# One scale for w_out, batch 0 kept in 32-bit pairs, and PSUM as three shared double banks: attention over packed rows with a SoLU layer

## The chip, the core and the metric

The program runs on one core of a Trainium2 chip. The metric is the time of one execution on the device in microseconds (us), taken as the median of several runs. The engines are named as in the profile: PE is the matmul engine (PEld its weight loads), DVE is VectorE, ACT is ScalarE, POOL is GpSimd, SP issues the DMAs.

## The reference

```python
# q, k, v: (8, 8, 576, 64); p: (8, 8, 32, 64); w_in: (512, 1024); w_out: (1024, 512)
def sm_attn(qq, kk, vv):
    s = scale * np.matmul(qq, kk.transpose(0, 1, 3, 2))
    s = s - np.max(s, axis=-1, keepdims=True)
    a = np.exp(s)
    a = a / (np.sum(a, axis=-1, keepdims=True) + 1e-09)
    return np.matmul(a, vv)
p_packed = sm_attn(p, k, v)              # 32 packed rows for each head
out = sm_attn(q, p_packed, p_packed)     # 576 rows for each head
x = out.transpose(0, 2, 1, 3).reshape(4608, 512)
h = x @ w_in
e = np.exp(h - max(h)); solu = h * e / (sum(e) + 1e-09)
ln = (solu - mean(solu)) / np.sqrt(var(solu) + 1e-06) * g_ln
return ln @ w_out
```

## The kernel before

**Units.** The work of a batch b is cut into flows: `k{b}` (`pack`: scores of the 32 packed rows of each head against the 576 keys, softmax, product with v), `q{b}` (`unpack`: scores of the 576 queries against the packed rows, softmax), and `z{b}` (`make_z`: packed rows times w_in, so that h = a · z needs no x of its own). Tokens are handled in 36 tiles of 128, `t0` to `t35` (`token_tile`): h from 12 matmuls of 512 columns (three for each half of the heads and each half of the columns), row maximum, exponential, the product u, the LayerNorm moments, a transpose by DMA, 24 matmuls into `po`, and the scaling by `c_row` on the way out. Tile 4 of each pair of batches is shared: 64 rows of the even batch and 64 of the odd one, whose matmuls use 64 columns of the array each.

**Numbers.** Products are made from pairs of parts (high·high, high·low, low·high). From batch 1 on the parts are 16-bit (`a_h`, `a_l`, `zh`, `zl`). Batch 0 uses 32-bit pairs (`a_r`, `z_r`) in its first four tiles, since the sizes that the 16-bit scales need are not known so early; for its last 64 rows, in `t4`, flow `y0` (`halves_of_z`) makes 16-bit parts of z afterwards, and `unpack` makes 16-bit parts of the last 64 columns of a.

**Weights.** w_in and w_out arrive as 64-bit words; `W0` to `W3` and `O0` to `O3` rebuild them as 32-bit numbers on ACT, DVE and POOL. For w_out each of the eight parts of 128 rows also gives `mag`, |g · w|, which PE sums over all rows with ones into one bank of 512 columns. `S` (`column_scale`) turns those 512 sums into a scale for each column, and `C0` to `C7` (`scaled_parts`) multiply w_out by g and the scale (DVE), cast the high part (ACT, `wch`) and subtract for the low part (POOL, `wcl`). `N` sizes w_in and `H` (`weight_halves`) makes its 16-bit parts for batches 2 to 7.

**PSUM.** There are eight banks: `ps_h` two tiles of two banks (h of the token tiles, all of batch 0, `p`), `ps_a` three tiles of one bank (scores, transposes and z of batches 1 to 7), `ps_o` one bank (`po`).

**Order.** Each flow is a generator; `ORDER` is a written list of 1372 names, and each name lets its flow issue the next step. Every engine runs its instructions in that order. SP's queue holds all DMAs in that order too. `SCALED_BY`, `E1T_BY` and their like are strings that choose an engine for an operation (a: ACT, d or x: DVE, p or g: POOL).

## Time and profile before

| | |
|---|---|
| median of 3 runs | 406.47 us (406.39 to 407.71) |
| the profiled execution | 406.56 us, of which the span of the instructions is 404.3 us |
| PE busy | 388.4 us (96%) |
| DVE, ACT, POOL busy | 310.4 us (77%), 266.3 us (66%), 241.1 us (60%) |
| granted clock of PE, mean | 0.996 of full speed |

The span is shorter than the time of its execution by 2.2 us, which lie around it. Busy times are of one execution. Matmuls overlap, so PE's busy time is no sum of their durations: 512 columns of 16-bit numbers show 0.38 us and start 0.21 to 0.22 us apart.

### The profile page before, as it was taken

The page shows a single profiled execution, that of the slowest core. Times are in us where ns is not written, and L with a number is a line of the kernel's source. Part 1 is how long each engine was busy: PE and PEld are TensorE (multiplying, and loading weights), DVE is VectorE, ACT ScalarE, POOL GpSimd, SP SyncE. Part 2 cuts the span into 40 slices and gives each one's busy share as a digit, 9 for nine tenths or more (in the row PEclk, how much of TensorE's full clock was granted, in tenths as well). Part 3 has the DMA queues.
Part 4 walks back from the last instruction along what each step waited for, and adds up shares of the span by engine and source line. Part 5 has one row for each costly group of instructions (what it writes and reads, how often), then busy time and mean ns, then how long its engine had stood idle before and what let it go on. Part 6 is the DMA issues. An engine that isn't in the chain of part 4 may idle for free.

```text
span 404.3 us, 8920 instructions
## 1 busy us (share of the span) xinstructions
PE 388.4 (96%) x3378; PEld 196.7 (49%) x3378; DVE 310.4 (77%) x550; ACT 266.3 (66%) x486; POOL 241.1 (60%) x423
## 2 busy tenths in 40 slices
PE   8988988999899999999999999999999999999996
PEld 8764655543433554345345444554455444444445
DVE  0265799999999989877998798888688787566631
ACT  2678998978677764685486844874476566754720
POOL 1442776665647886494548656663487568854450
PEclk9989999999999999999999999999999999999999
DMA  8999792779799995899896879863765354443661
GB/s 297 375 359 346 214 163 44 139 149 198 151 199 175 195 158 111 162 213 191 150 209 131 163 137 219 143 136 83 149 180 109 79 109 100 104 99 80 110 152 56
DMA packets 213865, 66.11 MB, mean 163 GB/s; under 512 B 194744, under 2 KB 207808, under 8 KB 213312
## 3 DMA queue, kind: packets, MB, share of 16 engines
q1 hardware_dynamic: 213824, 65.56, 74.3%
q8 instruction: 26, 0.43, 0.4%
q14 instruction: 15, 0.12, 0.1%
HBM read 37.23 MB, written 9.44 MB: 115 GB/s over the span
## 4 chain that ended last, share of the span: by engine, by line
PE 70%; DVE 12%; ACT 6%; POOL 4%; DMA 3%; SPq 2%; issue 2%; DVEq 0%; POOLq 0%; ACTq 0%
PE po L717 34%; PE h L662 17%; PE h L717 5%; DMA yT<-yhl 2%; PE po L116 2%; SPq L152 2%; PE pa L567 2%; PE pa L504 2%; PE pa L394 2%; DVE u L687 1%; PE pa L424 1%; PE pa L434 1%; ACT u L235 1%; ACT mag L255 1%; DVE kT L377 1%
## 5 line engine op out<-in xcount | busy, mean ns | idle before, releaser
L717 PE MATMUL po<-wch,yT 128*128 128x512 f16 x512 | 160.4, 380 | 0.2 <-DMA yT<-yhl 0.2
L717 PEld LDWEIGHTS <-yT 128*128 128x128 f16 x888 | 84.8, 98 | 103.9 <-issue 9.3
L717 PE MATMUL po<-wcl,yT 128*128 128x512 f16 x256 | 97.1, 379 | 0.0
L687 DVE SCALAR_TENSOR_TENSOR u<-e,s_row,h 128x1024 f32<-128x1024 f32 x36 | 45.8, 1271 | 16.8 <-ACT e L683 7.4
L693 ACT ACTIVATE yhl<-u,negmu 128x1024 f16<-128x1024 f32 x36 | 41.3, 1147 | 21.6 <-POOL negmu L690 21.4
L695 DVE SCALAR_TENSOR_TENSOR yhl<-u,negmu,yhl 128x1024 f16<-128x1024 f32 x36 | 46.3, 1286 | 5.6 <-ACT yhl L693 5.6
L665 DVE TENSOR_REDUCE nm<-h 128x1 f32<-128x1024 f32 x36 | 43.8, 1215 | 7.7 <-PE h L662 7.6
L662 PE MATMUL h<-zl,a_h 128*128 128x512 f16 (+1 forms) x160 | 47.9, 380 | 0.1
L683 ACT ACTIVATE e<-h,nmc,z_scale 128x1024 f32<-128x1024 f32 x32 | 38.4, 1201 | 7.8 <-DVE nmc L668 7.1
L701 ACT ACTIVATE e<-u,negmu 128x1024 f32<-128x1024 f32 x36 | 41.0, 1139 | 0.0
L673 POOL TENSOR_SCALAR bound<-nm,z_scale 128x1 f32<-128x1 f32 x31 | 17.9, 576 | 38.1 <-DVE nm L665 37.1
L662 PEld LDWEIGHTS <-a_h 128*128 128x128 f16 (+1 forms) x288 | 24.1, 101 | 31.5 <-issue 7.7
L662 PE MATMUL h<-zh,a_h 128*128 128x512 f16 (+1 forms) x128 | 38.3, 381 | 0.0
L670 ACT ACTIVATE nmc<-nm,z_scale 128x1 f32<-128x1 f32 x29 | 8.5, 295 | 39.4 <-DVE nm L665 39.2
L722 DVE SCALAR_TENSOR_TENSOR o_sb<-po,c_row,inv 128x512 f32<-128x512 f32 x32 | 23.9, 746 | 12.6 <-PE po L717 8.5
L662 PE MATMUL h<-zl,a_l 128*128 128x512 f16 (+1 forms) x80 | 30.3, 379 | 0.0
L709 POOL TENSOR_TENSOR c_row<-c_row,neg_half 128x1 f32<-128x1 f32 x36 | 23.8, 662 | 3.0
L662 PE MATMUL h<-zh,a_l 128*128 128x512 f16 (+1 forms) x64 | 24.3, 379 | 0.0
L679 POOL TENSOR_TENSOR s_row<-bound,neg_one 128x1 f32<-128x1 f32 x33 | 22.0, 667 | 2.7
L690 POOL TENSOR_SCALAR negmu<-su 128x1 f32<-128x1 f32 x36 | 7.4, 205 | 26.2 <-DVE u L687 22.6
L409 ACT ACTIVATE e<-pa,nmx 128x288 f32<-128x288 f32 x28 | 13.7, 493 | 12.5 <-DVE nmx L400 12.5
L475 POOL TENSOR_TENSOR s<-s,mx 128x576 f32<-128x576 f32 x14 | 17.7, 1278 | 7.0 <-DVE mx L473 6.8
(187 smaller groups left out, 747.2 us busy)
## 6 DMA issues: line engine op xcount, KB each, us to landing
out_dram<-o_sb SPq DMA_DIRECT2D x35, 256.0 KB, 2.6
v_sb<-in_v_dram SPq DMA_DIRECT2D x8, 1024.0 KB, 7.0
raw<-in_k_dram SPq DMA_DIRECT2D x24, 288.0 KB, 4.3
raw<-in_q_dram SPq DMA_DIRECT2D x96, 72.0 KB, 2.5
zl<-in_moe_w_in_dram SPq DMA_DIRECT2D x2, 1024.0 KB, 8.1
zh<-in_moe_w_in_dram SPq DMA_DIRECT2D x2, 1024.0 KB, 8.1
raw<-in_k_dram SPq DMA_DIRECT2D x2, 1024.0 KB, 9.7
raw<-in_q_dram SPq DMA_DIRECT2D x2, 1024.0 KB, 7.5
```

Source lines behind the costliest of these rows:

```text
L662: nc.tensor.matmul(dst_[:, cols], lhsT=lhsT, rhs=z[:, r, cols], start=bool(first), stop=bool(last))
L665: nc.vector.tensor_reduce(out=nm, in_=h, axis=AX.X, op=ALU.max, negate=True)
L673: by.tensor_scalar(out=bound, in0=nm, scalar1=-1.0 / U_MAX, scalar2=sc[:, :1], op0=ALU.mult, op1=ALU.max)
L679: nc.gpsimd.tensor_tensor(out=s_row, in0=bound, in1=neg_one, op=ALU.pow)
L683: nc.scalar.activation(e, h, AF.Exp, bias=nmc, scale=sc[:, 1:], accum_out=se)
L687: nc.vector.scalar_tensor_tensor(out=u, in0=e, scalar=s_row, in1=h, op0=ALU.mult, op1=ALU.mult, accum_out=su)
L693: nc.scalar.activation(yhl[:, 0], u, AF.Identity, bias=negmu)
L695: nc.vector.scalar_tensor_tensor(out=yhl[:, 1], in0=u, scalar=negmu, in1=yhl[:, 0], op0=ALU.add, op1=ALU.subtract)
L701: nc.scalar.activation(e, u, AF.Square, bias=negmu, accum_out=sq)
L709: nc.gpsimd.tensor_tensor(out=c_row, in0=c_row, in1=neg_half, op=ALU.pow)
L717: nc.tensor.matmul(po[:, cols], lhsT=yT[:, a, c], rhs=w[:, c, cols], start=c == 0 and t == 0, stop=c == NFC - 1 and t == 2)
L722: nc.vector.scalar_tensor_tensor(out=o_sb[:, cols], in0=po[:, cols], scalar=c_row, in1=inv[:, cols], op0=ALU.mult, op1=ALU.mult)
```

## The change

- **One scale for w_out.** `mag` becomes a Square on ACT with a sum over its row (`ssq`); the eight matmuls into the shared bank go. `S` sums the eight columns of `ssq` by one small matmul and gets one scale (a power of two) for the whole of w_out; `gs` is g times it, `inv` one number for each partition instead of 512. `C`: ACT makes `wch` straight from w with the scale in it, POOL multiplies w by `gs` and subtracts; DVE has no part in it.
- **Batch 0 in 32-bit pairs to its end.** `t4` uses `a_r` and `z_r` for the 64 rows of batch 0; `y0`, the 16-bit parts of a's last columns and batch 0's size go. `a_r` grows from 512 to 576 columns. `H` puts its high parts into the two buffers of `a_r` (so it follows `t4`'s products) and its low parts in place into w_in; `zh` and `zl` have both buffers for z again.
- **PSUM.** `ps_h` has three tiles of two banks, `ps_a` one bank. Scores, row transposes and z of all batches take a `ps_h` tile.
- **Score rows in `pack`.** One maximum and one exponential over both halves (2 × 288) instead of two of each; two small reduces for each row go. The transposes of the exponentials are evicted as 8 and 2 blocks instead of 4, 4 and 2, always by ACT; those of batch 1's q and k two groups at a time.
- **ORDER** is a new list of 1308 names. What the removed steps leave stays in about the same sequence; among the differences: the w_in part 2 and the keys of batch 0 are loaded first, w_out's part 0 earlier, `H` and `t4` change places.

```diff
-SCALED_BY = 'xxxxxxxx'
+SCALED_BY = 'gggggggg'
-E1T_BY = 'dadaaaaaa'
+E1T_BY = 'aaaaaa'
...
-    ps_h = ctx.enter_context(tc.tile_pool(name='ps_h', bufs=2, space=PSUM))
+    ps_h = ctx.enter_context(tc.tile_pool(name='ps_h', bufs=3, space=PSUM))
-    ps_a = ctx.enter_context(tc.tile_pool(name='ps_a', bufs=3, space=PSUM))
+    ps_a = ctx.enter_context(tc.tile_pool(name='ps_a', bufs=1, space=PSUM))
-    inv = const.tile([P, DM], F32, name='inv')
+    inv = const.tile([P, 1], F32, name='inv')
-    a_r = [par.tile([P, 2, MAIN], F32R, name=f'a_r{i}') for i in range(2)]
+    a_r = [par.tile([P, 2, S], F32R, name='a_r', bufs=2) for i in range(2)]
...
     def convert_w_out(n):
-            nc.tensor.matmul(sums[0], lhsT=ones, rhs=mag, start=len(sums) == 1, stop=len(sums) == NFC)
+            nc.scalar.activation(mag, t[:, i * DM:(i + 1) * DM], AF.Square, scale=g_sb[:, c:c + 1], accum_out=ssq[:, c:c + 1])
...
+    def size_of(dst, parts):
+        ps = ps_a.tile([P, 512], F32, name='pa')
+        n = parts.shape[-1]
+        nc.tensor.matmul(ps[:, :n], lhsT=ones_f, rhs=parts, start=True, stop=True)
+        yield
+        nc.vector.tensor_reduce(out=dst, in_=ps[:, :n], axis=AX.X, op=ALU.add)
+        half_exponent(dst, dst)
+    def w_out_scale():
+        yield from size_of(inv, ssq)
+        up = small.tile([P, 1], F32, name='up')
+        nc.vector.tensor_scalar(out=up.bitcast(I32), in0=inv.bitcast(I32), scalar1=-1, scalar2=204 << 23, op0=ALU.mult, op1=ALU.add)
+        yield
+        nc.vector.tensor_scalar_mul(gs, g_sb, up)
+        nc.vector.tensor_scalar(out=inv.bitcast(I32), in0=inv.bitcast(I32), scalar1=65 << 23, scalar2=None, op0=ALU.add)
...
     def scaled_parts(c):
-            nc.vector.scalar_tensor_tensor(out=w, in0=w, scalar=g_sb[:, c:c + 1], in1=scale[0], op0=ALU.mult, op1=ALU.mult)
...
-        nc.scalar.copy(wch[:, c], w)
...
-        EN(nc, REST_BY[c]).tensor_tensor(out=wcl[:, c], in0=w, in1=wch[:, c], op=ALU.subtract)
+            nc.scalar.activation(wch[:, c], w, AF.Copy, scale=by)
...
+                nc.gpsimd.tensor_scalar(out=w, in0=w, scalar1=by, scalar2=0.0, op0=ALU.mult, op1=ALU.add)
...
+            nc.gpsimd.tensor_tensor(out=wcl[:, c], in0=w, in1=wch[:, c], op=ALU.subtract)
...
     def weight_halves():
+        hi = [par.tile([P, 4 * S], F16, name='a_r', bufs=2)[:, :2 * DF].rearrange('p (g f) -> p g f', g=2) for _ in range(2)]
+        halves.append([hi[g // 2][:, g % 2] for g in range(G)])
+        halves.append([w_in_sb[:, g].bitcast(F16)[:, :DF] for g in range(G)])
...
     def pair(b):
+        t = ps_h.tile([P, DF], F32, name='h')
+        return [t[:, :512], t[:, 512:], t]
...
     def transpose_rows(dst, raw, b, by, m0):
-        wide = 1 if b else 2
+        wide = 2
...
     def pack(b):
+                both = s1[2].rearrange('p (n x) -> p n x', n=2)[:, :, :HALF]
+                nc.vector.tensor_reduce(out=nmx, in_=both, axis=AX.XY, op=ALU.max, negate=True)
+                yield
...
+                nc.scalar.activation(dst, both if by_rows else both.rearrange('p n (a t) -> p n a t', t=32), AF.Exp, bias=nmx, accum_out=ssum[:, r:r + 1])
...
-        for i0 in range(0, len(items), 4):
-            grp = items[i0:i0 + 4]
+        for i0 in range(0, len(items), 8):
+            grp = items[i0:i0 + 8]
+            pt = ps_h.tile([P, DF], F32, name='h') if len(grp) > 4 else ps_a.tile([P, 512], F32, name='pa')
...
     def unpack(b):
-                parts = [(a_r[0][:, r], a_r[1][:, r], a2T[:, :MAIN]), (a_h[0][:, r, MAIN:], a_l[0][:, r, MAIN:], a2T[:, MAIN:])]
+            hi, lo = (a_h[b % 2][:, r], a_l[b % 2][:, r]) if b else (a_r[0][:, r], a_r[1][:, r])
...
-    def halves_of_z():
...
     def token_tile(i, dst, b, c):
+                        a_hi, a_lo, z_hi, z_lo = (a_h[x], a_l[x], zh[c + x], zl[c + x]) if c + x else (a_r[0], a_r[1], z_r[0], z_r[1])
...
-            nc.vector.scalar_tensor_tensor(out=o_sb[:, cols], in0=po[:, cols], scalar=c_row, in1=inv[:, cols], op0=ALU.mult, op1=ALU.mult)
+            nc.vector.tensor_scalar(out=o_sb[:, cols], in0=po[:, cols], scalar1=c_row, scalar2=inv, op0=ALU.mult, op1=ALU.mult)
```

## Rows read from the trace of the kernel before

**Rows 1.** Windows: us, busy of PE, PEld, DVE, ACT, POOL; PEclk, DMA share, GB/s.

```profile
20.00:40.00 20.00, 16.27 (x255) 11.49 (x257) 11.62 (x24) 16.09 (x29) 7.38 (x3) 0.91 1.06 353
40.00:56.00 16.00, 14.09 (x184) 8.91 (x185) 13.01 (x24) 15.88 (x29) 11.50 (x7) 1.00 0.87 198
56.00:78.00 22.00, 19.84 (x221) 12.58 (x216) 21.76 (x43) 20.27 (x45) 15.17 (x18) 1.00 0.62 102
78.00:131.00 53.00, 50.76 (x449) 21.71 (x441) 51.80 (x97) 40.70 (x74) 31.94 (x59) 1.00 0.90 173
131.00:380.00 249.00, 248.70 (x2018) 114.30 (x2011) 200.89 (x352) 158.43 (x293) 160.81 (x303) 1.00 0.70 141
```

**Rows 2.** Instructions of PE in order of time: start, duration, count at the end.

```profile
56.61 0.50 PE L662 MATMUL h<-zh,a_r 128*128 128x512 f32 x1
...
76.86 0.40 PE L662 MATMUL h<-zl,a_r 128*128 128x512 f32 x1
77.10 0.40 PE L662 MATMUL h<-zh,a_r 128*128 128x512 f32 x1
...
78.07 0.39 PE L717 MATMUL po<-wch,yT 128*128 128x512 f16 x1
...
103.06 0.38 PE L662 MATMUL h<-zh,a_h 128*64 128x512 f16 x1
103.06 0.38 PE L662 MATMUL h<-zl,a_h 128*64 128x512 f16 x1
...
232.34 0.59 PE L662 MATMUL h<-zh,a_h 128*128 128x512 f16 x2
```

**Rows 3.** Whom PE waited for from 40 to 131 us: total, times, longest.

```profile
PE pa L441 <- DVE pp L438: 1.8, 2, 1.2
```

**Rows 4.** Groups of PE: busy us, mean ns of one.

```profile
L259 PE MATMUL po<-mag,ones 128*128 128x512 f32 x8 | 4.0, 501 | 1.6 <-ACT mag L255 1.5
```

**Rows 5.** Groups of ACT: busy us, mean ns of one.

```profile
L409 ACT ACTIVATE e<-pa,nmx 128x288 f32<-128x288 f32 x28 | 13.7, 493 | 12.5 <-DVE nmx L400 12.5
L409 ACT ACTIVATION_READ_ACCUMULATOR e<-pa,nmx 128x1 f32 x28 | 5.5, 197 | 0.0
L366 ACT COPY kT<-h 128x1024 f32<-128x1024 f32 x1 | 1.0, 1012 | 3.3 <-PE h L364 3.3
```

**Rows 6.** Groups of DVE: busy us, mean ns of one.

```profile
L695 DVE SCALAR_TENSOR_TENSOR yhl<-u,negmu,yhl 128x1024 f16<-128x1024 f32 x36 | 46.3, 1286 | 5.6 <-ACT yhl L693 5.6
L473 DVE TENSOR_REDUCE mx<-s 128x18 f32<-128x576 f32 x16 | 11.6, 738 | 0.0
L398 DVE TENSOR_REDUCE mx<-pa 128x1 f32<-128x288 f32 x28 | 11.3, 445 | 1.8 <-PE pa L394 1.7
L636 DVE SCALAR_TENSOR_TENSOR zh<-zf,z_scale,zh 128x512 f16<-128x512 f32 x4 | 4.1, 1058 | 0.0
L289 DVE SCALAR_TENSOR_TENSOR yT<-yT,g_sb,po 128x512 f32<-128x512 f32 x4 | 3.0, 740 | 0.0
L400 DVE TENSOR_REDUCE nmx<-mx 128x1 f32<-128x2 f32 x16 | 2.5, 155 | 0.5
L525 DVE TENSOR_TENSOR a_l<-s,a_h 128x64 f16<-128x64 f32 x2 | 1.4, 707 | 0.0
L270 DVE TENSOR_SCALAR po<-po 128x512 f32<-128x512 f32 x1 | 0.7, 700 | 0.1
```

**Rows 7.** Groups of POOL: busy us, mean ns of one.

```profile
L690 POOL TENSOR_SCALAR negmu<-su 128x1 f32<-128x1 f32 x36 | 7.4, 205 | 26.2 <-DVE u L687 22.6 <-DVE s_p L543 3.2 <-DVE ssum L411 0.4
L297 POOL TENSOR_TENSOR wcl<-yT,wch 128x512 f16<-128x512 f32 x4 | 5.5, 1372 | 2.3 <-ACT wch L295 2.3
```

**Rows 8.** Instructions of DVE in order of time, two places.

```profile
97.91 1.77 DVE L636 SCALAR_TENSOR_TENSOR zh<-zf,z_scale,zh 128x512 f16<-128x512 f32 x1
...
238.67 1.28 DVE L687 SCALAR_TENSOR_TENSOR u<-e,s_row,h 128x1024 f32<-128x1024 f32 x1
```

**Rows 9.** An instruction of POOL in order of time.

```profile
96.95 2.18 POOL L525 TENSOR_TENSOR a_l<-s,a_h 128x576 f16<-128x576 f32 x1 [2.35 <-ACT a_h L522]
```

More of the change, by code (lines that the diff above doesn't have):

```diff
@@ L110, in packed_attention_solu_kernel @@
     size, weight, whole, halves = ({}, [], {}, [])
-    got, packed, wg, sums, scale = ({}, {}, {}, [], [])
+    got, packed, wg = ({}, {}, {})
     spare = ps_o.tile([P, DM], F32, name='po')
@@ L180, in prepare_g @@
         yield
-        nc.scalar.copy(g_sb, spare[:, :NFC])
+        nc.scalar.activation(g_sb, spare[:, :NFC], AF.Copy, scale=2.0 ** (-16))
         yield
@@ L313, in weight_size @@
             yield
-        ps = ps_a.tile([P, 512], F32, name='pa')
-        nc.tensor.matmul(ps[:, :G], lhsT=ones_f, rhs=sums_, start=True, stop=True)
-        yield
         w = const.tile([P, 1], F32, name='w_size')
-        nc.vector.tensor_reduce(out=w, in_=ps[:, :G], axis=AX.X, op=ALU.add)
-        half_exponent(w, w)
+        yield from size_of(w, sums_)
         nc.vector.tensor_scalar(out=w.bitcast(I32), in0=w.bitcast(I32), scalar1=-1, scalar2=235 << 23, op0=ALU.mult, op1=ALU.add)
@@ L343, in bank @@
     def bank(b):
-        return ps_a.tile([P, 512], F32, name='pa') if b else ps_h.tile([P, DF], F32, name='h')
+        return ps_h.tile([P, DF], F32, name='h')
     def pair(b):
-        if b == 0:
-            t = bank(b)
-            return [t[:, :512], t[:, 512:]]
-        return [bank(b), bank(b)]
+        t = ps_h.tile([P, DF], F32, name='h')
+        return [t[:, :512], t[:, 512:], t]
     def transpose_rows(dst, raw, b, by, m0):
@@ L445, in pack @@
         yield
+        if not b:
+            return
         squares = att.tile([P, 2 * D], F32, name='squares')
@@ L492, in unpack @@
             for r in range(2):
[L493 removed]
+                for n, bank_ in enumerate(pair(b)[:2]):
                     for out_, lhsT, rhs in scores(bank_, r, n):
@@ L555, in product @@
         def product(n):
-            in_h = not b or Z_IN_H[b] == str(n + 1)
-            if in_h:
-                banks[n] = pair(0)
+            banks[n] = pair(0)[:2]
             cols = slice(512 * n, 512 * n + 512)
             if ZP_BY[b] == '1':
-                if not in_h:
-                    banks[n] = [bank(b), bank(b)]
                 for t, (x, y) in enumerate(((0, 0), (0, 1), (1, 0))):
@@ L566, in product @@
                         for g in range(G):
-                            nc.tensor.matmul(banks[n][r][32 * g:32 * g + 32, :], lhsT=pph[rows, x, 32 * g:32 * g + 32], rhs=halves[y][rows, g, cols], start=t == 0, stop=t == 2)
+                            nc.tensor.matmul(banks[n][r][32 * g:32 * g + 32, :], lhsT=pph[rows, x, 32 * g:32 * g + 32], rhs=halves[y][g][rows, cols], start=t == 0, stop=t == 2)
                 yield
@@ L570, in product @@
             for r in range(2):
-                if not in_h:
-                    banks[n].append(bank(b))
                 rows = slice(64 * r, 64 * r + 64)
@@ L617, in make_z @@
                     yield from part(n)
-    def halves_of_z():
-        z_scale(0)
-        s_z = zsc[0][:, :1]
-        parts = par.tile([P, 2, 2, DF], F16, name='zh', bufs=2)
-        zh[0], zl[0] = (parts[:, 0], parts[:, 1])
-        if 0 not in whole:
-            whole[0] = par.tile([P, 2, DF], F32, name='zf')
-        yield
-        for n in range(2):
-            for r in range(2):
-                cols = slice(512 * n, 512 * n + 512)
-                if ZF_BY[0] == 'l':
-                    nc.gpsimd.tensor_tensor(out=whole[0][:, r, cols], in0=z_r[0].bitcast(F32)[:, r, cols], in1=z_r[1].bitcast(F32)[:, r, cols], op=ALU.add)
-                    yield
-                nc.scalar.activation(zh[0][:, r, cols], whole[0][:, r, cols], AF.Copy, scale=s_z)
-                yield
-                nc.vector.scalar_tensor_tensor(out=zl[0][:, r, cols], in0=whole[0][:, r, cols], scalar=s_z, in1=zh[0][:, r, cols], op0=ALU.mult, op1=ALU.subtract)
-                yield
     def token_tile(i, dst, b, c):
```

84 lines of the change are left out of this document (29 added, 55 removed).

## The prediction

> **What bounds the kernel now.** I read the windows first, to split the span into stages, then PE's waits, then the groups of each engine. After 131 us nothing is left to gain around PE: it is busy 248.70 of 249 us there, so that stage can only become longer, or shorter by the work taken from PE [rows 1]. What can be won lies before. Between 40 and 56 us ACT is full (15.88 of 16), and between 56 and 131 DVE is (21.76 and 51.80 of 75 us, together 73.56); ACT has 60.97 there, POOL 47.11 [rows 1]. PE's idle time is 3.73 us in 20 to 40, 1.91 in 40 to 56, 2.16 in 56 to 78 and 2.24 in 78 to 131 [rows 1]. The first two stages end with the first matmul of the first token tile at 56.61; the first of an output product comes at 78.07 [rows 2]. The longest of PE's waits after 40 us is for DVE's `pp` [rows 3], a 64-column operation behind a full queue, which agrees with DVE as the limit. PE's idle time is a lower bound of what a faster DVE returns, because a matmul shows 0.38 us and the next can start after some 0.22; short waits hide in that.
>
> **The change, part by part.**
>
> *The sums of w_out.* Eight matmuls with 4.0 us of busy time go from PE [rows 4]; one small one comes. They all lie between 32 and 49 us, where PE has idle time and ACT and the loads set the pace, so the removal is worth between 0 (idle time takes their place) and 4.0 (PE had been the limit). DVE loses the three operations of `S` on 512 columns, 3 × 0.70 = 2.1 us [rows 6], and gets eight small ones of at most 0.155 each, 1.2 us.
>
> *ACT before the first tile.* The squares cost what the magnitudes did, plus the read of the accumulator: 8 × 0.197 = 1.6 us more [rows 5]. The eviction of batch 0's transposed exponentials moves from DVE: one copy of 1.01 in place of one half as wide, and a narrow one of at most 0.5, together about 1.0 more. Gone are the copy of `inv` (0.5, half as wide as the 1.01 row), two narrow casts and batch 0's size with its read (four short instructions, 0.8 at 0.197 each), and in each of its two score rows two exponentials with their reads, 2 × (0.493 + 0.197) = 1.38 us, for one of 576 columns that costs between 0.69 and 2 × 0.493 + 0.197 = 1.18 [rows 5]: 0.4 to 1.4 less for both. Added up, +2.6 against −1.7 to −2.7: ACT, the full engine of that stage, gets no lighter. I take 1.0 us for the whole stage, near the lower end of 0 to 4.0, for DVE's relief (most of `S` and the two copies) and for a third double bank, which lets `p`, k, q and z of batch 0 overlap.
>
> *DVE from 56 to 131.* Five of the eight products of `C` start after 57 us: 5 × 0.74 = 3.7. `y0` has 4.1 and its scale 0.3. The narrow subtraction of a has up to 1.2 of the 1.4 shown for two; its columns, added to the wide one, cost 0.1 at most. Four score rows lie in there: two reduces of 0.445 and two small ones of about 0.15 each become one; for one over 576 columns the nearest row is 0.738, so 1.19 − 0.74 = 0.45 less, and nothing less if PSUM in two pieces costs as much as two reduces. 4 × 0.45 = 1.8 at most; I take 1.0 [rows 6]. Together 3.7 + 4.4 + 1.1 + 1.0 = 10.2 us of 73.56, leaving 63.4 of 75, or 84%. In the stage after 131 DVE works at 200.89 of 249, 81%, and PE hardly waits [rows 1]. So DVE ceases to be the limit. What it can return is the idle 2.16 + 2.24 = 4.4 us.
>
> *POOL from 56 to 78.* The multiplication by `gs` goes to POOL, eight times. No row shows a POOL operation of 512 columns with one tensor; it costs between the 0.205 of one column and the 1.372 of two tensors of 512 [rows 7], so 1.6 to 11.0 us. All eight must precede the end of the first output product, and behind them in POOL's queue stand `bound` and `negmu` of the first tiles, for which ACT and DVE wait. POOL has 22 − 15.17 = 6.83 us free in this stage [rows 1]: it is full from 0.85 us each on. I take 0.8, the middle, so 6.4 us: it just fits, with no slack, and I take 0.8 off the 4.4 us for it. That leaves 3.6.
>
> The Trainium skill has a page price for this: by GPSIMD Engine Reference, section 3.1, 512 elements through the one-tensor loop were measured at 769 ns, which gives an estimate of 6.2 us for the eight; no run here shows it, and by it POOL would have 0.6 us left, and the sum would stay.
>
> *Tile 4.* Its two halves now start side by side as 16-bit matmuls of 64 columns (both at 103.06). Batch 0's half becomes a 32-bit one, for which 0.24 us pass to the next start [rows 2], against 0.21 of a 16-bit one. If they still run side by side, 12 × 0.03 = 0.4 us more; if not, 12 × 0.24 = 2.9. I take 0.4: the array's columns stay apart.
>
> *PSUM after 131.* A token tile holds its double bank from its first matmul (232.34) until u has been read (238.67 + 1.28 = 239.95): 7.6 us [rows 2, 8]. Per batch there are 4.5 tiles, 34 us, and now on the same three double banks two score rows, two z halves, two query scores and one eviction; at about 2.5 us each, 18 us. That is 52 of 3 × 41 us (a batch takes 4.5 × 9.2, from 27 tiles in 249 us): 42% full. I take 0.2 us of waits, with 0 as the lower end. The written order of the tail gives the last tiles about the same cover as before; 0.
>
> *Hidden at nothing.* `H` in place and into `a_r`: the same instructions, after `t4`'s products; z2 is not needed until some 40 us later. `o_sb` with two scalars instead of a row: 512 columns from PSUM at 0.70 as in `S` [rows 6]. The halves' old buffers only add freedom. SP's queue carries the same loads; w_out's part 1 must wait in it until ACT has read a part of w_in, with v behind it, but the DMA share of 1.06 says that the engines have a backlog to cover that [rows 1].
>
> **Sum.** 1.0 + 3.6 − 0.4 − 0.2 = 4.0 us less than the 406.56 of the profiled execution, 402.6; the median lies 0.1 lower, so 402.5. Its own range, from 0.5 of the 4.4 idle us lost or 2 us of hidden waits gained: 400.5 to 405.2.
>
> **Rivals.** A change under 1.2 us (0.3% of 406.47, or 405.25 to 407.69) can't be told from none.
>
> *Rival 1, all of it comes back.* PE runs without a gap from the first tile on and the first tile comes earlier by the PE time removed: 4.0 + 4.4 − 0.4 = 8.0 us less, 398.5. For it: DVE's 84%. Against: ACT's 15.88 of 16, and three engines near full until 78 us. Chance 0.20.
>
> *Rival 2, POOL takes DVE's place.* At 1.2 us each the multiplications need 9.6 of the 6.83 free us; the first output product slides by 2.8, and the tiles behind it with it. Besides, a DVE operation with two SBUF tensors runs longer beside POOL: `y0`'s took 1.77 us beside `a_l` of POOL, which ran from 96.95 to 99.13, and 1.06 in the mean, against 0.74 for an operation of the same width with one input in PSUM [rows 6, 8, 9]. Some eight `yhl` of DVE, all with two SBUF tensors, fall from 56 to 131; 8 × 0.32 = 2.6 us. The gain of 4.0 then is eaten by about 2.8 + 0.5: 405.8. It decides from 0.85 us an operation. Chance 0.16. By the Trainium skill this is a rule (SBUF — State Buffer, section "Who interferes with whom": a DVE instruction with two SBUF inputs contends with a GpSimd instruction that reads SBUF, whoever issues first holds the shared ports for the whole instruction); the trace agrees with its 1.77 us.
>
> *Rival 3, PSUM becomes the bound (slower).* One place: `ps_h`. PE's order is fixed, so a score row or a z half that finds all three double banks held stops everything behind it. If each of the seven takers of a batch waits 0.2 us, batches 2 to 7 lose 6 × 7 × 0.2 = 8.4 us: 406.5 − 4.0 + 8.4 = 410.9. It decides from 0.1 us a taker, 4.2 us. Against: 42% full. For it: before, these takers had three banks of their own. Chance 0.16.
>
> That the change doesn't do what it says is no case here: each part removes named instructions.
>
> **How the numbers follow.** The forecast has 0.48, the rivals 0.20, 0.16 and 0.16. Faster: forecast and rival 1, with a little of rival 2: 0.70. Within 0.3%: the rest of rival 2 and rival 3's lower end: 0.15. Slower: 0.15. For the range I leave out 0.09 below, half of rival 1, and 0.11 above, most of rival 3: 398.4 to 407.4.
>
> **What would show it.** DVE under 90% between 56 and 131 us, with PE's idle time there under 1.5 us (the main term); the first tile's first matmul at 55 to 56.6 us; the first output product at 74 to 76.5; POOL's multiplications near 0.8 us; tile 4's halves still starting in pairs; PE over 99% after 131 with no wait of an `h` for a reader of PSUM. The prediction is wrong if POOL is the full engine between 56 and 78 and the first output product does not come earlier than 77, if PE shows repeated waits after 131, or if the first tile comes later than 57 because ACT's new sequence of squares and w_in parts delays batch 0's scores.

## The result and the profile after

The changed kernel takes 401.57 us (median of 4 runs, 400.77 to 402.90) beside 406.43 for the kernel before: ratio 0.9862, 95% interval 0.9817 to 0.9907 (the quotient of the two medians, 0.988, lies inside it). Its profiled execution took 401.95 us with a span of 400.2. The forecast was 402.5. As will be seen, the time came out right by luck: errors of the sum, of opposite signs, nearly cancel.

The windows of the changed kernel, with the columns of [rows 1]:

```profile
20.00:40.00 20.00, 15.78 (x245) 11.14 (x246) 8.08 (x15) 15.78 (x26) 9.05 (x4) 0.83 0.93 310
40.00:56.00 16.00, 12.99 (x176) 10.38 (x174) 11.68 (x22) 15.64 (x28) 12.00 (x9) 0.79 1.15 194
56.00:78.00 22.00, 20.81 (x236) 14.09 (x232) 21.29 (x34) 21.72 (x41) 20.27 (x25) 1.00 1.10 179
78.00:131.00 53.00, 52.48 (x439) 23.53 (x438) 48.75 (x86) 37.44 (x63) 33.76 (x60) 1.00 0.90 165
131.00:380.00 249.00, 248.19 (x2028) 118.06 (x2027) 200.54 (x320) 155.53 (x270) 164.25 (x305) 1.00 0.74 141
```

PE's idle time from 56 to 131 us fell from 4.40 to 1.71 us. DVE is still busy for 70.0 of those 75 us (93%), and from 56 to 78 ACT (21.72) and POOL (20.27) are as full as DVE. PE's clock is new: it stood at half (1.2 of 2.4 GHz) for about 6.8 us in each of the first two windows (0.83 of 20 us, 0.79 of 16), 13.6 us in all, where before it was 3.6 [rows 1]. This holds for one execution. The other three of the changed kernel have a mean granted clock of 0.991 against its 0.983, which makes about 7 us at half (an estimate). And experiment 4 below, which is the same up to w_out's parts, kept the clock whole in the second window:

```profile
40.00:56.00 16.00, 11.52 (x182) 8.05 (x168) 12.12 (x23) 15.84 (x29) 12.35 (x9) 1.00 1.02 195
```

PE of the changed kernel in order of time; these are the marks of [rows 2]:

```profile
58.17 0.50 PE L633 MATMUL h<-zh,a_r 128*128 128x512 f32 x1
...
76.52 0.39 PE L688 MATMUL po<-wch,yT 128*128 128x512 f16 x1
...
93.94 0.58 PE L633 MATMUL h<-zh,a_r 128*64 128x512 f32 x1
94.45 0.40 PE L633 MATMUL h<-zl,a_h 128*64 128x512 f16 x1
94.79 0.45 PE L633 MATMUL h<-zl,a_r 128*64 128x512 f32 x1
95.17 0.40 PE L633 MATMUL h<-zl,a_h 128*64 128x512 f16 x1
95.50 0.45 PE L633 MATMUL h<-zh,a_r 128*64 128x512 f32 x1
```

The first tile starts 1.6 us later than before, the first output product 1.6 us earlier. The first mark is not firm: the kernels of experiments 1, 2, 6 and 7, which are the same up to there, have it at 57.59, 57.53, 58.16 and 57.41. From 93.94 on stands `t4`: 32-bit and 16-bit products take turns, each starting 0.33 to 0.38 us behind the last. The 24 products take 8.7 us (to 102.64); the later shared tiles, whose halves start in pairs, take 2.71.

Marks of two kernels with different orders hold different amounts of work. So here the PE work still to come is set beside each mark: an estimate, in which each remaining product counts with the distance to the next start that its kind shows (0.216 us for 512 columns of 16 bits, for instance; tile 4's products count in both kernels as halves that start in pairs). With other means for the kinds the differences move by up to 0.5 us.

```
mark (us)                            before  after   PE work left: before, after   gain by then
first tile's first product            56.6    58.2         332.7, 331.6              -0.5
first output product                  78.1    76.5         315.2, 315.1              +1.7
third tile's first output product     93.7    91.5         299.7, 298.5              +3.4
sixth tile's first output product    131.1   129.0         265.5, 266.8              +0.8
26th tile's first output product     320.4   316.2          79.4,  79.3              +4.3
last product's end                   401.1   397.0           0                       +4.1
```

So the first stage loses a little or nothing (0.5 here, less with the earlier starts just named), 56 to 92 us returns 3.9, 92 to 131 loses 2.6 (`t4` stands there), and behind 131, where I expected nothing, 3.5 us are gained.

Whom PE waited for in the first 135 us:

```profile
PE h L385 <- ACT pT L207: 3.1, 1, 3.1
PE h L355 <- DMA raw<-in_k_dram: 1.9, 1, 1.9
PE h L201 <- ACT pT L207: 1.6, 1, 1.6
...
PE pa L440 <- DVE pp L437: 0.7, 1, 0.7
```

The long wait for DVE's `pp` [rows 3] is down to 0.7 us. The largest is new: batch 0's second score row (L385, from 23.2 to 26.3 us) waits for a copy of `pT`. In ACT's order of time the cause stands ahead of it; the last row is of SP's queue:

```profile
22.86 1.12 ACT L221 ACTIVATE e<-zh 128x1024 f32<-128x1024 f32 x1 [2.18 <-DMA zh<-in_moe_w_in_dram]
...
25.71 0.57 ACT L207 ACTIVATE pT<-h 128x512 f32<-128x512 f32 x1
```

```profile
25.12 0.39 SPq L168 DMA_DIRECT2D zh<-in_moe_w_out_dram  x1
```

ACT stood for w_in's part 0 until 22.86 with the copy behind it; and SP could issue w_out's part 1 only at 25.12, when ACT had read that part, with v behind it in the queue. The window around it shows the DMA engines at a share of 0.29 and 45 GB/s, where the whole stretch of 20 to 40 us has 0.93 and 310:

```profile
24.00:27.00 3.00, 0.67 (x8) 0.40 (x12) 1.36 (x2) 3.00 (x7) 1.83 (x1) 0.81 0.29 45
```

### The profile page after: what moved, and what is told of

It reads as the page before. It is cut to its first block, busy times and chain, and to the rows that moved or that the text cites. A ratio compares the mean times of both kernels' runs of the same rounds, so it can differ in the third digit from the quotient of the medians.

```text
span 400.2 us, 8803 instructions
## 1 busy us (share of the span) xinstructions
PE 383.8 (96%) x3370; PEld 202.3 (51%) x3370; DVE 300.4 (75%) x485; ACT 259.4 (65%) x443; POOL 249.1 (62%) x431
## 4 chain that ended last, share of the span: by engine, by line
PE 82%; DMA 9%; ACT 3%; DVE 2%; SPq 1%; issue 1%; DVEq 0%; ACTq 0%
PE po L688 39%; PE h L633 23%; PE h L688 5%; DMA raw<-in_k_dram 5%; PE h L355 4%; DMA zh<-in_moe_w_in_dram 3%; PE h L385 3%; PE h L559 2%; PE h L505 2%; PE h L423 2%; PE pa L433 2%; DMA yT<-yhl 1%; ACT e L654 1%; DVE u L658 1%; SPq L151 1%
## 5 line engine op out<-in xcount | busy, mean ns | idle before, releaser
L688 PEld LDWEIGHTS <-yT 128*128 128x128 f16 x888 | 85.9, 98 | 100.3 <-issue 3.8
L666 DVE SCALAR_TENSOR_TENSOR yhl<-u,negmu,yhl 128x1024 f16<-128x1024 f32 x36 | 48.4, 1347 | 2.7 <-ACT yhl L664 2.5
L644 POOL TENSOR_SCALAR bound<-nm,z_scale 128x1 f32<-128x1 f32 x31 | 15.8, 511 | 44.7 <-DVE nm L636 39.7
L693 DVE TENSOR_SCALAR o_sb<-po,c_row,inv 128x512 f32<-128x512 f32 x32 | 25.8, 808 | 19.3 <-PE po L688 16.3
L633 PE MATMUL h<-zh,a_h 128*128 128x512 f16 (+1 forms) x120 | 35.8, 380 | 0.0
L242 POOL TENSOR_TENSOR w_in_sb<-w_in_sb,u 128x1024 int32<-128x1024 int32 x4 | 9.5, 2379 | 26.2 <-ACT u L234 13.9
L633 PE MATMUL h<-zh,a_l 128*128 128x512 f16 (+1 forms) x60 | 22.7, 379 | 0.0
L355 PE MATMUL h<-ident,raw 128*64 128x128 f32 x256 | 19.6, 321 | 1.9 <-DMA raw<-in_k_dram 1.9
L650 POOL TENSOR_TENSOR s_row<-bound,neg_one 128x1 f32<-128x1 f32 x33 | 19.5, 592 | 2.7
L688 PE MATMUL h<-wch,yT 128*128 128x512 f16 (+1 forms) x80 | 20.4, 336 | 0.7 <-DVE o_sb L693 0.7
```

The costliest lines, as they stand in the source:

```text
L355: nc.tensor.matmul(pt[64 * r:64 * r + 64, g * MAIN + c * P:g * MAIN + (c + 1) * P], lhsT=rows[:, c, 2 * (g0 + g) + r], rhs=ident, start=Tr ...
L633: nc.tensor.matmul(dst_[:, cols], lhsT=lhsT, rhs=z[:, r, cols], start=bool(first), stop=bool(last))
L650: nc.gpsimd.tensor_tensor(out=s_row, in0=bound, in1=neg_one, op=ALU.pow)
L666: nc.vector.scalar_tensor_tensor(out=yhl[:, 1], in0=u, scalar=negmu, in1=yhl[:, 0], op0=ALU.add, op1=ALU.subtract)
L688: nc.tensor.matmul(po[:, cols], lhsT=yT[:, a, c], rhs=w[:, c, cols], start=c == 0 and t == 0, stop=c == NFC - 1 and t == 2)
L693: nc.vector.tensor_scalar(out=o_sb[:, cols], in0=po[:, cols], scalar1=c_row, scalar2=inv, op0=ALU.mult, op1=ALU.mult)
```

## The experiments

All were timed beside the kernel before; each ratio is to that kernel, with its 95% interval. To compare them with the changed kernel, I take the difference of the ratios, times 406.5 us. The changed kernel's own interval is 1.8 us to either side, and with the quotient of its medians it would lie 0.7 us nearer to the kernel before, so differences under about 2 us are read from the traces, not from the times. A good measure there is the stretch from the first tile's first product to the last product's end, which leaves the scatter of the first stage out: 338.8 us in the changed kernel.

**1. The first shared tile's terms grouped by batch.**

```diff
-            for r in range(2):
-                for t in range(3):
-                    for x in range(2):
+            for x in range(2):
+                for r in range(2):
+                    for t in range(3):
```

> The changed kernel with one edit: in the first shared tile (and the three later ones) the terms run over the batch first, so that the six products of one half, in 32-bit pairs, stand together and the six of the other half, in 16-bit parts, behind them. Theory: it is the alternation of the two data types that costs, 24 products in 8.7 us; grouped, each takes its own 0.21 to 0.24 us and the 24 take about 5.4 us, and the kernel gains 2.5 to 3.5 us (about 398.5 us). The three later shared tiles, all 16-bit, lose their pairing: 2.6 us become about 5.2 us in each, which takes 7 to 8 us back, so that the whole kernel should come out 4 to 5 us slower than the changed kernel (about 406 us); what decides is the stretch of the first shared tile. Rival: a 64-column product costs 0.36 us wherever it stands beside the other half; then the first shared tile's 24 products still take about 8.7 us.

400.83 us, ratio 0.9842 (0.9816 to 0.9868). The tile's 24 products took 6.14 us in place of 8.70: inside a group they start 0.22 to 0.23 us apart, and each of the three changes of kind costs about 0.1 more. The first rival falls. One part of the expectation was wrong: the later tiles, all 16-bit, took 3.17 us and not 5.2. Products of the two halves still start 0.03 us apart there, although they are issued six by six. So 2.6 us were won in the first shared tile and 0.5 lost in each of the other three. So it is not the issue order that keeps two halves from running together; two kinds don't, two of one kind do.

**2. Both halves of the first shared tile 16-bit.**

```diff
-... = (a_h[x], a_l[x], zh[c + x], zl[c + x]) if c + x else (a_r[0], a_r[1], z_r[0], z_r[1])
+... = (a_h[x], a_l[x], zh[c + x], zl[c + x]) if c else (a_h[1], a_l[1], zh[1], zl[1])
```

> The changed kernel with one edit: in the first shared tile the half that belongs to batch 0 is computed from batch 1's 16-bit parts instead of batch 0's 32-bit pairs, so that 64 rows of the output are other numbers; the products are as many and as wide. Theory: the two halves of one type run side by side again, the 24 products take about 2.7 us instead of 8.7 us, and the kernel gains 5 to 6 us (about 396 us). Rival: what the tile loses is covered by a wait that would come anyway (the engines behind it are the bound), and less than 1 us comes back.

398.98 us, ratio 0.9800 (0.9777 to 0.9824), 2.5 us less than the changed kernel. PE in order of time, the tile's second half:

```profile
97.09 0.41 PE L633 MATMUL h<-zl,a_l 128*64 128x512 f16 x2 [0.73 <-POOL a_l L521]
97.33 0.60 PE L633 MATMUL h<-zl,a_h 128*64 128x512 f16 x4
97.76 0.38 PE L633 MATMUL h<-zl,a_l 128*64 128x512 f16 x2
```

The products run in pairs again. The tile took 4.49 us and not 2.7, since it stood twice for POOL's `a_l` of batch 1 (1.4 us by PE's waits); in the changed kernel no such wait shows. So 4.2 us came back in the tile and some 2.5 to 3 at the end.

**3. Another order of the first loads.**

```diff
-'Z lw2 lk0 lg lw1 W1 W1 k0 g W1 lp k0 lo0 g O0 k0 O0 k0 lp O0 lw3 W2 p lw0 p W1 ... W0 k0 W0 W0 O0 W0 ...'
+'lw1 Z lk0 lg lw2 W1 W1 k0 g W1 lp k0 lw0 g W0 k0 W0 k0 lp W0 lw3 W2 p lo0 p W1 ... O0 k0 O0 O0 W0 O0 ...'
```

> The changed kernel with the order of its first loads changed: block 1 of w_in is loaded first instead of third, and block 0 of w_in before the first part of w_out, with the two conversions swapped in the order to match. Theory: the first stage lost its time because ScalarE, which works in order, stood until 12.2 us and again until 22.9 us for two blocks of w_in, and the transfers stood nearly still at 22 to 25 us behind a buffer that it freed late; with both gone the first tile's first product comes at 55.5 to 57 us instead of 58.2 and the kernel gains 1 to 2.5 us (about 400 us). Rival: the first stage is bound by the transfers' sum, and another block comes late in place of these: the first tile's first product stays at 58 us or later, no gain.

403.04 us, ratio 0.9897 (0.9873 to 0.9921): no gain. The theory falls. ACT's waits for w_in shrank to 3.4 and 0.5 us, and SP issued w_out's part 1 at 20.4 us; but now ACT waited 1.94 us for w_out's part 0, until 23.12, with the same copy of `pT` behind it. PE waited 3.5 us for it, and the first tile started at 58.98. The rival was right: another block comes late in its place.

**4. w_out's low parts on DVE instead of POOL.**

```diff
-SCALED_BY = 'gggggggg'
+SCALED_BY = 'dddddddd'
```

> The changed kernel with the low parts of the scaled w_out made by one VectorE instruction each, eight in all, in place of two GpSimd instructions each. Theory: VectorE is the scarcer of the two before 131 us; eight instructions of about 0.7 us put 5 to 6 us on it, of which a third to a half shows: 1 to 3 us slower (about 403.5 us). Rival: GpSimd has become the bound of 56 to 78 us (20.3 of 22 us busy) and takes VectorE's port besides; without its 16 instructions the kernel is 1 us or more faster.

405.27 us, ratio 0.9960 (0.9939 to 0.9981): 4.0 us of the gain gone (3.7 in the stretch behind the first tile's start), more than either expected. Its window, and the new group of DVE (it has a second of four like it):

```profile
56.00:78.00 22.00, 18.23 (x215) 12.01 (x210) 20.31 (x37) 19.51 (x36) 3.76 (x7) 1.00 0.87 154
```

```profile
L288 DVE SCALAR_TENSOR_TENSOR wcl<-yhl,gs,wch 128x512 f16<-128x512 f32 x4 | 3.0, 745 | 1.6 <-ACT wch L285 1.6
```

POOL was nearly empty, and yet PE was busy 2.6 us less in this stage and the first output product slid from 76.5 to 79.1. DVE is what this stage hangs on, and POOL has not taken its place. But 4.0 us is not the price of 5.9 us of work alone. In front of the first `wcl` DVE also stood 1.6 us for ACT's `wch` (the row above), where all its waits in this window were 0.4 in the changed kernel. And with POOL idle beside it, the first tile's `yhl` got shorter:

```profile
71.24 1.28 DVE L666 SCALAR_TENSOR_TENSOR yhl<-u,negmu,yhl 128x1024 f16<-128x1024 f32 x1
```

1.28 us instead of 2.27 (its row in the changed kernel is shown further down). What the work alone costs was not separated.

**5. A copy of `pT` ahead of w_in's part 0.**

```diff
-... W2 p p p W0 k0 W0 W0 O0 W0 p p k0 k0 k0 k0 p lo1 ...
+... W2 p p p p p W0 k0 W0 W0 O0 W0 k0 k0 k0 k0 p lo1 ...
```

> The changed kernel with one move in the order: the copy of p's third block and the fourth block's products stand ahead of the conversion of block 0 of w_in on ScalarE, not behind it. The loads stay as the changed kernel has them. Theory: the 3.1 us that TensorE stood at 23 us hang on this copy, which ScalarE reaches only when it has waited for that block; with the move the wait goes, the second score row comes 2 to 3 us earlier, the first tile's first product comes at 56 to 57 us instead of 58.2, and the kernel gains 1 to 2 us (about 400 us). Rival: the transfers' gap at 22 to 25 us is what delays the stage (v and the next blocks land late), then the first tile stays at 58 us and nothing is gained.

401.13 us, ratio 0.9847 (0.9808 to 0.9886): not to be told from the changed kernel. The wait of 3.1 us went, as expected; but PE then waited 3.3 us for the exponential's release of a bank and 1.5 us for v, and the first tile started at 57.86. So neither this copy nor the loads alone set this stage: each wait that goes uncovers the next.

**6. The first shared tile in two blocks, the others in pairs.** First batch 0's 12 products over both column halves, then batch 1's.

```diff
+        if b is None and not c:
+            steps = [[(n, x) for n in range(NH) for x in terms[6 * i:6 * i + 6]] for i in range(2)]
...
```

> The changed kernel with the first shared tile's 24 products in two blocks: first the 12 of batch 0's half (32-bit pairs), then the 12 of batch 1's (16-bit), over both column halves; the later shared tiles keep their pairs. Theory: two kinds never run side by side, so it is the sum of both, 24 times 0.22 us, and two changes of kind: 5.4 to 5.8 us in place of 8.7, about 2 us less than the changed kernel (399.5 us). Rival: the first experiment's gain of the tile was given back later and here too; no gain over it (400.8 us).

398.61 us, ratio 0.9783 (0.9749 to 0.9816): 3.2 us less than the changed kernel. PE at the change of kind:

```profile
96.78 0.40 PE L637 MATMUL h<-zh,a_r 128*64 128x512 f32 x1
97.11 0.62 PE L637 MATMUL h<-zl,a_h 128*64 128x512 f16 x2
97.56 0.38 PE L637 MATMUL h<-zl,a_l 128*64 128x512 f16 x1
```

The tile took 5.75 us (94.06 to 99.81, where the next product starts), 2.95 less, and all of it reached the end of the kernel: the span is 2.9 shorter. The one change of kind costs 0.33 instead of 0.22 us.

**7. Bursts of 32-column products kept apart.** A score row, a z half or a query score is a burst of 32-column products side by side. In PE's order of time I counted how often a product of 32 columns follows one of 64 or 128: behind 131 us 30 times before, 14 times after, since the new order puts such bursts next to each other. One of them before, alone between 128-column products:

```profile
208.62 0.38 PE L717 MATMUL po<-wch,yT 128*128 128x512 f16 x1
208.93 0.72 PE L394 MATMUL pa<-kT,pT 64*32 64x288 f32 x16
209.58 0.61 PE L662 MATMUL h<-zl,a_h 128*128 128x512 f16 x2
```

Three of them in the changed kernel, and the way out of one:

```profile
225.99 0.38 PE L688 MATMUL po<-wch,yT 128*128 128x512 f16 x1
226.30 0.72 PE L505 MATMUL h<-qT,ppT 64*32 64x288 f32 x16
226.81 0.69 PE L385 MATMUL h<-kT,pT 64*32 64x288 f32 x16
227.30 0.42 PE L559 MATMUL h<-a_r,pph 64*32 64x512 f16 x8
...
228.12 0.72 PE L505 MATMUL h<-qT,ppT 64*32 64x288 f32 x16
228.77 0.39 PE L688 MATMUL po<-wch,yT 128*128 128x512 f16 x1
```

From a 128-column product into a burst 0.31 us pass, where 0.21 to 0.22 are the rule; a score burst followed by a product takes 0.65 us and one followed by another burst 0.51. Together about 0.23 us for each way in and out: 16 fewer are 3.7 us, an estimate at the price of a score row, and somewhat less where the burst is a z half (its last product and a 128-column one start 0.31 us apart, with another burst behind it 0.24). The experiment puts a product of one column between such neighbours.

```diff
+    def part_bursts(b, spot):
+        if burst[0] and b > 1:
+            nc.tensor.matmul(spot, lhsT=wch[:, 0, :P], rhs=wch[:, 0, :1], start=True, stop=True)
+        burst[0] = True
...
```

> The changed kernel with one product of a single column (128 by 128, 16-bit, into a column that nothing reads) ahead of each burst of 32-column products from batch 2 on that would follow another such burst directly: 24 of them. Theory: what the kernel gained behind 131 us came from such bursts standing together (TensorE enters them 14 times there, 30 before), since entering from a 128-column product took 0.31 us instead of 0.21 and leaving 0.335 instead of 0.196: 24 times 0.23 us and the product itself, 5 to 7 us slower than the changed kernel (about 407.5 us). Rival: the gain there came from the PSUM banks or from the lighter VectorE, and the added products cost no more than their own few hundredths, under 1.5 us in all.

407.02 us, ratio 0.9982 (0.9959 to 1.0005): 4.9 us of the gain gone, and 5.5 in the stretch behind the first tile's start. The same place in its order of time:

```profile
228.53 0.72 PE L519 MATMUL h<-qT,ppT 64*32 64x288 f32 x16
229.18 0.18 PE L340 MATMUL h<-wch 128*128 128x1 f16 x1
229.29 0.71 PE L393 MATMUL h<-kT,pT 64*32 64x288 f32 x16
229.94 0.18 PE L340 MATMUL h<-wch 128*128 128x1 f16 x1
230.04 0.41 PE L574 MATMUL h<-a_r,pph 64*32 64x512 f16 x8
```

From burst to burst it is now 0.76 and 0.75 us instead of 0.51 and 0.49: 0.25 each, 24 times 6.1, of which some 0.1 each is the added product itself. The rival falls: a break between bursts has the price that the rows show. That the changed kernel's gain behind 131 us is made of the 16 breaks fewer follows from this price and the count; the kernel before with its bursts put together was not run.

**8. One scale for w_out alone, in the kernel before.** The diff's edits of `convert_w_out`, `S`, `C`, `g_sb`, `inv` and `o_sb`, in the old order; where the eight sums stood, nothing.

> The kernel before with the first part of the change alone: one scale for the whole of w_out from sums of squares, ScalarE and GpSimd making the parts, its own order, its own PSUM and its own batch 0. Theory: the 10 us that this takes off VectorE are what its stage up to 131 us waits for, and the 4.0 us of column sums leave TensorE: 2.5 to 4 us faster than the kernel before (about 403 us). Rival: the gain of the changed kernel hangs on its new order and on batch 0, and this part alone, put into the old order, gives less than 1 us.

412.56 us, ratio 1.0119 (1.0078 to 1.0159): slower than the kernel before by 4.8 us, where both expected a gain. Two of its windows:

```profile
40.00:56.00 16.00, 14.42 (x158) 10.35 (x158) 9.88 (x20) 13.48 (x26) 10.41 (x7) 0.74 0.91 188
56.00:78.00 22.00, 19.23 (x177) 12.90 (x177) 15.19 (x31) 19.09 (x43) 18.73 (x20) 0.84 0.72 78
```

DVE is light now (15.19 of 22), but only because the tiles' work comes later: from 78 to 131 us it is busy 52.31 of 53. The first tile starts at 61.70. The granted clock fell to half for 20.5 us before 78 us. The eight removed products had stood just where PE waits, so I took the clock for the cause. The times speak against it: two of the six executions, with a mean granted clock of 0.991 and 0.992, still took 410.8 and 411.0 us.

**9. The same with the eight products kept.**

```diff
+            nc.tensor.matmul(sums[0], lhsT=ones, rhs=mag, start=len(sums) == 1, stop=len(sums) == NFC)
```

> The kernel of the eighth experiment (the kernel before with one scale for w_out) with the eight products of the column sums put back on TensorE at their old places, on the squares; nothing reads what they give. Theory: the part alone lost 5 us because those eight products had kept TensorE at work while it waited; without them its clock stood at half speed for 20.5 us before 78 us instead of 3.4. With them back, half speed lasts under 5 us, the first tile's first product comes at 56 to 57.5 us instead of 61.7, and the kernel takes about 403.5 us (402.5 to 405), 9 us less than the eighth. Rival: the loss came from ScalarE's longer squares, the accumulators' reads and GpSimd's sixteen instructions in an order that was not made for them; then the products add 4 us of work and the kernel stays at 410 us or more.

414.27 us, ratio 1.0162 (1.0126 to 1.0199). The theory falls: from 40 to 56 us the clock was whole again, half speed lasted some 10 us in all, and the first tile started no earlier, at 61.96. What holds it is read from PE's waits and ACT's order of time:

```profile
PE pa L398 <- ACT kT L370: 1.9, 1, 1.9
```

```profile
55.47 1.33 ACT L293 ACTIVATE wch<-yhl,gs 128x512 f16<-128x512 f32 x2 [1.39 <-DVE inv L280]
```

Batch 1's first scores wait for ACT's copies of `kT`. These come later since ACT reads eight accumulators more (0.19 us each) and stands 1.39 us for the scale, which `wch` now needs. Before, `wch` came behind DVE's product, and the old order has no room for the scale's wait. That these two make up the loss was not tested. Nor is it all: in the traces of both experiments 6 us are lost by the sixth tile's first output product, and some 2 more behind it, where PE waits for the transposed `yT` (2.6 and 1.9 us).

**10. PE kept at work in the first stage.** Experiment 6 with 29 products of constants ahead of five waits.

```diff
+            fill(12 * (b == 0 and r == 1))
...
+    def fill(n):
+        for _ in range(n):
+            nc.tensor.matmul(spare, lhsT=ones, rhs=ones.unsqueeze(1).broadcast_to([P, DM // P, P]), start=True, stop=True)
...
```

> The kernel of the sixth experiment (the changed kernel with the first shared tile's products in two blocks) with 29 products of constants, 512 columns each, put on TensorE where it stands waiting for another engine before 44 us: 5, 12, 3, 4 and 5 of them. They give nothing that is read. Theory: after each of those waits the granted clock was half for 3.4 to 6.8 us; with TensorE at work in them it stays whole, batch 0's and batch 1's first products there take half as long, the first tile's first product comes 1 to 1.5 us earlier (56.5 to 57 us), and the kernel gains 0.7 to 1.5 us on the sixth (about 397.5 us). Rival: the stage waits for ScalarE's order and for the loads anyway, so the faster products only wait longer: the same within 0.4 us, or slower where the added products stand in the way.

398.18 us, ratio 0.9774 (0.9743 to 0.9806): 0.4 us under experiment 6, which the times can't tell from nothing; the span is 1.0 shorter. Its first windows:

```profile
20.00:40.00 20.00, 18.73 (x284) 12.89 (x288) 9.81 (x17) 17.87 (x29) 10.50 (x5) 1.00 0.93 317
40.00:56.00 16.00, 13.74 (x194) 9.67 (x186) 12.24 (x21) 15.89 (x29) 12.82 (x8) 1.00 1.24 201
```

The clock stayed whole (its mean is 1.000 in this execution and 0.994 to 1.000 in all six, 0.983 to 0.990 in those of experiment 6), and the first tile started at 55.90 and the first output product at 74.3, both 2.3 us earlier than in experiment 6 (1.5 earlier than the earliest start without the products, 57.41). The theory's mechanism holds, its price not: the second tile's first output product comes at 83.1 instead of 83.5, the third's at 90.6 instead of 91.6, and the end 1.0 earlier in the span. More than half of what the first stage gains is given back by 83 us; from 56 to 78 us DVE, ACT and POOL are all nearly full there (20.87, 20.44 and 19.97 of 22).

**11. The score row's two halves apart again.**

```diff
-                nc.vector.tensor_reduce(out=nmx, in_=both, axis=AX.XY, op=ALU.max, negate=True)
...
+                for n in range(2):
+                    nc.vector.tensor_reduce(out=mx2[:, n:n + 1], in_=s1[n][:, :HALF], axis=AX.X, op=ALU.max)
+                nc.vector.tensor_reduce(out=nmx, in_=mx2, axis=AX.X, op=ALU.max, negate=True)
...
+                for n in range(2):
+                    nc.scalar.activation(dst[:, n], src[:, n], AF.Exp, bias=nmx, accum_out=es[:, n:n + 1])
+                nc.vector.tensor_reduce(out=ssum[:, r:r + 1], in_=es, axis=AX.X, op=ALU.add)
```

> The changed kernel with the score row's maximum and exponential taken over the two halves apart again: two maxima and a small one, two exponentials and a small sum, as in the kernel before; the order and PSUM as in the changed kernel. By the rows this puts about 0.44 us on VectorE and as much on ScalarE for each of 16 rows, six of them before 131 us. Theory: VectorE is what the stage before 131 us waits for, so of 2.6 us a third to a half shows: 0.8 to 1.3 us slower than the changed kernel (about 402.6 us). Rival: with VectorE at 92 per cent it absorbs this, and the difference is under 0.4 us.

410.14 us, ratio 1.0074 (1.0044 to 1.0103): 8.6 us slower than the changed kernel, far beyond both. One row of DVE's waits tells why:

```profile
DVE ssum L400 <- ACT e L399: 18.1, 11, 3.1
```

My version put the small sum directly behind the exponentials, and DVE, which works in order, stood for ACT in front of it. It measured this stall, not the work.

**12. The same with the sum late.** One sum for both rows, just ahead of the reciprocal.

```diff
...
+        nc.vector.tensor_reduce(out=ssum, in_=sums2[b].rearrange('p (r n) -> p r n', n=2), axis=AX.X, op=ALU.add)
```

> As the eleventh experiment, but the small sum of the four exponentials' sums stands once for both rows, just ahead of the reciprocal that needs it, so that VectorE waits nowhere that it did not wait in the changed kernel. Theory: most of the eleventh's 8.5 us were VectorE standing still behind ScalarE (18.1 us in 11 waits for the exponential, ahead of the small sum), not the added work; by what 5.5 us of VectorE cost in the fourth experiment (3.6 us), the 2.2 us that are left before 131 us cost 1 to 1.6 us: about 402.9 us. Rival: it is the second exponential and its accumulator on ScalarE that delay the rows; then 5 us or more of the eleventh's loss remain (406 us or more).

402.60 us, ratio 0.9897 (0.9879 to 0.9914): 1.4 us over the changed kernel by the ratios, 1.0 by the medians. The times alone can't tell this from nothing, but the stretch behind the first tile's start is 1.2 us longer too, about as expected. 7 of the eleventh's 8.6 us were the stall. The edit adds work to ACT as well as to DVE, and which of the two the 1.2 us are was not separated.

## Why the prediction was right, and where its steps were not

**DVE's relief was the right mechanism.** The sum gave 3.6 us for 56 to 131. By the marks 3.9 came back up to 92 us, and PE's idle time fell by 2.7 us. Experiment 4 shows that the stage hangs on DVE: its work put back costs 4.0 us, part of which is DVE's own wait for ACT. What the third double bank and the new order give in this stage was not tested apart from it. But DVE did not become light: 93% and not 84%. Some of its instructions got longer (below); that a faster stage also draws in the next tiles' work is likely and was not counted. "DVE under 90%" failed; "PE's idle time under 1.5" just failed, at 1.71. And the relief did not work in the old order: there the same part made the kernel slower (experiments 8 and 9), and PE's waits point to ACT's queue. The prediction had costed the parts without the order.

**The first stage gave nothing.** I gave it +1.0; it lost 0.5 in the profiled execution, and with the starts of the kernels that are the same up to there, between 0.5 and nothing. By the prediction's own words this was a sign of being wrong: the first tile later than 57 because ACT's new sequence delays batch 0's scores. The first tile is later than 57 in all of them, and the rows show such a delay (L385 behind `pT` behind w_in's part 0). It is not the whole cause, since without this wait (experiment 5) the first tile still started at 57.86. "SP's queue ... a backlog to cover that" was wrong too: around 25 us the DMA engines ran nearly dry (0.29), because w_out's part 1 could not be issued before 25.12. The four score and exponential operations that I weighed show in none of these waits; the order of the loads against ACT's order does, and experiments 3 and 5 show that neither of the two changes of it made there sets the stage free. The prediction had no term for PE's clock, which stood at half for 13.6 us in this execution against 3.6. That the removed products of the sums had kept it up is not shown. Experiment 10 shows what a whole clock is worth here: 1.5 to 2.3 us in the stage, 0.4 to 1.0 at the end.

**Tile 4 was the mis-sized term.** "The array's columns stay apart" gave 0.4 us, with 2.9 as the upper bound. The products of a 32-bit and a 16-bit half don't run side by side, and each turn costs some 0.1 us more: 6.0 us, twice the bound. The bound had only the price of two kinds in a row, and no price of changing between them. Experiment 6 got 2.95 of them back by one rearrangement, all of it to the end.

**Behind 131 us there was something to gain.** "Nothing is left to gain around PE" was read from its 248.70 of 249 busy us. Busy time hides what a product pays for its neighbour: the overlapping 0.38 us of a product look the same at a distance of 0.21 and of 0.31. 16 fewer entries into 32-column bursts are worth 3.7 us by the rows; the marks show 3.5; splitting 24 cost 4.9. The Trainium skill says (TensorEngine Tiling (Array Packing), section "Key Properties") that changing the tiling mode drains TensorE, and that different tiles work in parallel. The trace agrees with the first, by its 0.31 against 0.21 us; with the second only where both tiles hold one data type.

**The rest.** POOL's multiplications were taken at 0.8 us; the two groups of four show

```profile
L291 POOL TENSOR_SCALAR yhl<-yhl,gs 128x512 f32<-128x512 f32 x4 | 3.7, 936 | 0.5 <-POOL yhl L254 0.5
L291 POOL TENSOR_SCALAR yT<-yT,gs 128x512 f32<-128x512 f32 x4 | 2.7, 690 | 0.4 <-ACT wch L285 0.4
```

6.4 us for the eight, as forecast, and POOL (20.27 of 22) just holds. The contention of rival 2 is there, in single instructions: POOL's and DVE's order of time show

```profile
69.32 1.67 POOL L291 TENSOR_SCALAR yhl<-yhl,gs 128x512 f32<-128x512 f32 x1
```

```profile
68.16 2.27 DVE L666 SCALAR_TENSOR_TENSOR yhl<-u,negmu,yhl 128x1024 f16<-128x1024 f32 x1
```

1.67 us against 0.69 to 0.70 for the other seven, and 2.27 against 1.286 in the mean before [rows 6] and 1.28 for the same instruction in experiment 4, where POOL was nearly empty. Only three of the 36 `yhl` of the changed kernel take over 2 us. Still, experiment 4 shows that moving this work back to DVE is worse. By the Trainium skill (SBUF — State Buffer, section "Who interferes with whom") a DVE instruction with two SBUF inputs contends with a POOL instruction that reads SBUF; these rows agree with it. A maximum over 576 columns of PSUM took 0.740 us (0.738 had been taken), an exponential 0.735. `o_sb` with two scalars, put at nothing for a row of 0.70, took 0.81 in the changed kernel and in experiment 8, against 0.75 with the row of scales: about 2 us of DVE in the whole kernel. Rival 3 did not come: behind 131 us PE waited twice, 0.8 and 0.7 us, for a reader of a `ps_h` bank, 1.5 in all for the 0.2 taken, and far from the 8.4 of the rival.

Term by term against the forecast, by the marks: the first stage -1.5 us (-0.5 for +1.0); tile 4 -5.6; the rest of 56 to 131 us +3.7 (3.9 up to 92 and 3.4 behind it, once tile 4's 6.0 are set apart, for 3.6); behind 131 us +3.7 (3.5 for -0.2). Together +0.3: the forecast held because these cancel, and that is luck. Some 0.4 us of the gain lie outside the span (2.2 us before, 1.8 after), for which no term stood. What makes up the 3.4 between 92 and 131 us was not taken apart; three entries into bursts fewer (4 for 7) are 0.7 of it. The upper end of the sum's own range, 405.2, can't be redone from its words: half of the 4.4 idle us lost gives 404.7.

## What to carry to other kernels

An engine that is busy for 99.9% of a stage may still be paying for the order of its work: read the distance between starts at each change of shape or type, and put products of one shape and type together. The relief of the full engine paid here in one order and not in another; price a part in the order in which it will run. Put a small instruction that needs another engine's result where that result is long there: placed too early it held DVE up, and the kernel lost 7 us (experiments 11 and 12). When a wait is removed, ask which instruction is next in that engine's queue: two of the experiments here (3 and 5) moved a wait and gained nothing.

## What was not expected of the hardware

- Two 64-column halves of a tile, one 32-bit and one 16-bit, never ran together: 24 products took 8.70 us taking turns, 5.75 us in two blocks; in the later shared tiles, where both are 16-bit, they took 2.71. With one type it hardly matters whether they are issued in turns or six by six (2.71 and 3.17 us).
- From 128-column products into a score row's burst of 32-column ones and out again costs about 0.23 us beyond the products themselves; a single one-column product between two bursts cost 0.25 us.
- PE's clock fell to half behind waits of 1.3 to 3.1 us (changed kernel and experiment 6), but not behind all: in experiment 4 it stayed whole behind one of 2.0 us, for the same load as one of 1.9 us in the changed kernel, behind which it fell. The 64 transposes of batch 1's keys behind that one took 6.28 us, where 32 of batch 0's had taken 1.97 us at full speed. Products of constants in those waits kept it whole (experiment 10), at no loss.
